# Second norm of an adaLN, attention and gated-MLP kernel: row groups 2 to 4 turned by VectorE block transposes and a trip through DRAM

## The chip, the cores and the metric

The kernel runs on one core of a Trainium2 chip. The metric is the device time of one execution in microseconds (us). The program is written by hand for five engines that each run their own queue in order: TensorE (PE: matmuls and transposes), VectorE (DVE), ScalarE (ACT), GpSimd (POOL) and SyncE (SP, which here issues nearly all DMA transfers). [...] PSUM is the memory that TensorE writes, SBUF the on-chip memory that all engines read, DRAM the memory outside.

## The reference, cut to what matters

Everything is fp32, with S = 2048 rows (tokens), D = 448 columns, 16 heads of 28, and FH = 896 hidden columns per half.

```python
mod = silu(c) @ w_mod                  # six parts of 448: sa, ca, ga, sb, cb, gb
h = layernorm(x) * (1 + ca) + sa       # first norm
x = x + ga * mha(h)                    # scores over all 2048 rows, softmax, wo
h = layernorm(x) * (1 + cb) + sb       # second norm
z = gelu(h @ w_in)                     # 2048 x 1792
z1, z2 = z[:, :896], layernorm(z[:, 896:])
g = w_sp @ z2 + b_sp[:, None]          # mixes the 2048 rows
x = x + gb * ((z1 * g) @ w_out)
```

## The kernel before, in words

An fp32 matmul is done as products of two fp32r parts: each operand is split into hi (a rounded copy, by ScalarE's `Copy`) and lo (the difference, by `sub`, L150). With D = 448, `h` transposed has 448 partitions' worth of rows in chunks of 128: chunks 0 to 2 have hi in slots 0 to 2 and lo in slots 3 to 5; the last 64 columns have hi in the lower and lo in the upper half of slot 6. For that, the last 64 columns are produced twice, in both halves of the partitions. A product over these slots is 11 matmuls, `STEPS`; its last two, `STEPS_Z = [(6, 6), (6, 7)]`, read slot 6.

The rows are handled as 16 tiles of 128 and 4 groups of 512 (`g`), four tiles each. The kernel goes through these stages: the first norm and the QKV products; attention; the output product wo; the second norm; z1 (the first half of h @ w_in, stored to DRAM); z2; the mix by w_sp; the gate and w_out (the y stage, where `x2_load`, L1508, fetches x back for the last addition).

The change lies between wo and z1. In this stretch there is no planner: the order of each engine's queue is the order in which the code calls the helpers, under a manual schedule.

- `x_load(g)` (L1037) loads a group of x, one DMA; the host lays out the inputs beforehand, so that partition p, tile t holds row g*512 + t*128 + p.
- `wo_tile(t)` is `wo_mm` (L830, 11 matmuls into PSUM) and `wo_add` (L1045, VectorE adds the product to x; L1046 stores the tile to `x2_scr`). For tiles 0 to 7 the two `STEPS_Z` matmuls and the add come later than the rest, in two loops.
- `h2_stats(g)` (L1054, L1058, L169, L170) takes mean and variance on VectorE and 1/sqrt(variance) on GpSimd.
- `h2_norm(g)` (L1066) normalises on VectorE, 448 columns and once more the last 64.
- `h2_group(g)` calls `ln_transpose`: 16 transposes on TensorE (L179, 4 chunks of 4 tiles), then for each chunk on ScalarE the scale and shift (L186, into `hfull`) and the hi copy (L193), and on VectorE the lo part (L150). The chunks are taken in the order 0, 2, 1, 3. `after(c)` is called behind each chunk.
- `z1_unit(g, f)` is 11 matmuls (L1158) into one PSUM bank, a gelu on ScalarE (L1162, which reads PSUM and writes one of four `z1t` slots), and a store (L1163). There are 28 units, four groups of seven; the units of group g read `h2T[g]`.
- `win_load` (L1074) and `win_prep` load and split w_in's second half for z2. `wout_load` (L1188), `wout_part` (L1192, L1194, L150) and `wout_store` (L1200) scale w_out by gb, split it and store it; for w_out chunk i they stand behind z1 units 10 + 2i, 11 + 2i and 12 + 2i.

The order is: statistics of groups 0 and 1, norm of group 0, tiles 8 to 11, norm of group 1, tile 12, transposes of group 0 (with tile 13 inside), tile 14, transposes of group 1 (with tile 15 and the statistics of group 2), norm of group 2, statistics of group 3, and the z1 units; group 2 is transposed behind unit 4, and group 3 behind unit 9.

## Time and profile before

| quantity | value |
|---|---|
| time of the kernel, median of 3 runs | 1376.16 us (1376.03 to 1377.29) |
| the profiled execution | 1376.63 us |
| its span in the profile | 1374.8 us |
| TensorE busy | 1368.6 us of the span |
| VectorE, ScalarE, GpSimd busy | 1112.7, 801.8, 359.6 us |
| moved by DMA | 254.32 MB, 185 GB/s on average |

The profile is of one execution. The span runs from its first to its last instruction, and the execution's own time is 1.8 us longer. Times within the trace are counted from the start of the span. A row that names an instruction has the line of the code, the engine, the operation, the tile written and the tiles read, and a count; "busy, mean ns" is the total time in us and the mean time of one, and what follows the second bar is the idle time of the engine ahead of these instructions with what ended it. In the chain of work and the timeline a row begins with the start and the duration in us. A row of a DMA queue has packets, MB, and the time they took as a share of all 16 DMA engines. PEclk is the clock granted to TensorE, in tenths, where 9 means 90% or more.

### The profile page before, as it was taken

What the parts mean: (1) busy time and instruction counts of PE and PEld (TensorE: products, weight loads), DVE (VectorE), ACT (ScalarE), POOL (GpSimd) and SP (SyncE); (2) the same over time, 40 slices, a digit from 0 to 9 for tenths busy, and PEclk for the clock granted to TensorE, in tenths of its full rate; (3) what the DMA queues carried; (4) which work ended last, traced back from release to release, by engine and by line L of the source; (5) the groups of instructions that cost most, each with busy time, mean ns of one, the idle gap of its engine ahead of it and who ended that gap; (6) DMA issues with size and microseconds to landing.
All of it is one profiled execution on the core that took longest, in us unless ns stands there. A gap on an engine that the chain in (4) does not pass through costs nothing.

```text
span 1374.8 us, 20854 instructions
## 1 busy us (share of the span) xinstructions
PE 1368.6 (100%) x7098; PEld 974.7 (71%) x7098; DVE 1112.7 (81%) x1771; ACT 801.8 (58%) x1471; POOL 359.6 (26%) x367
## 2 busy tenths in 40 slices
PE   9999999999999999999999999999999999999998
PEld 8888665556555655565556554888898888888898
DVE  7898899999999999999999981773367777999752
ACT  6623676767676767676767679364324544555420
POOL 2134335244535264745650012200011000000000
PEclk9999999999999999999999999999999999999999
DMA  8464756777677667776773110535604765788552
GB/s 289 137 175 176 233 158 214 201 221 229 210 218 209 209 203 237 234 224 214 231 221 103 32 44 23 177 139 179 225 20 142 233 203 184 249 283 267 180 183 90
DMA packets 137079, 254.32 MB, mean 185 GB/s; under 512 B 21832, under 2 KB 37322, under 8 KB 134426
## 3 DMA queue, kind: packets, MB, share of 16 engines
q1 hardware_dynamic: 134254, 248.79, 58.0%
q10 hardware_dynamic: 2718, 4.19, 0.8%
q8 instruction: 56, 0.92, 0.3%
q14 instruction: 51, 0.42, 0.1%
HBM read 174.53 MB, written 73.59 MB: 180 GB/s over the span
## 4 chain that ended last, share of the span: by engine, by line
PE 95%; DVE 2%; issue 2%; DMA 1%; POOL 0%; ACTq 0%; ACT 0%; DVEq 0%; POOLq 0%; SPq 0%
PE st_ps L743 18%; PE mt L711 17%; PE o_ps L758 16%; PE z_ps L1384 5%; PE acc L1453 5%; PE acc L1451 5%; PE acc L1452 5%; PE pq L406 5%; PE z_ps L1158 5%; PE pv L388 2%; PE y_ps L1518 2%; PE y_ps L1520 2%; PE y_ps L1519 2%; PE acc L1461 1%; PE acc L1459 1%
## 5 line engine op out<-in xcount | busy, mean ns | idle before, releaser
L716 DVE TENSOR_REDUCE pm<-mt 128x1 f32<-128x512 f32 x1024 | 627.4, 678 | 7.8 <-PE mt L711 7.8
L747 ACT ACTIVATE P<-st_ps 128x512 f32<-128x512 f32 x1024 | 512.6, 644 | 203.4 <-PE st_ps L743 200.9
L743 PE MATMUL st_ps<-qst,kst 128*128 128x512 f32 x1024 | 409.6, 410 | 0.0
L711 PE MATMUL mt<-kst,qst 128*128 128x512 f32 x1024 | 401.6, 392 | 0.0
L743 PEld LDWEIGHTS st_ps<-qst,kst 128*128 128x128 f32 x1024 | 191.2, 188 | 138.9 <-DVE pm L716 65.1
L758 PE MATMUL o_ps<-P,V 128*32 128x512 f32 x2048 | 240.0, 597 | 0.0
L711 PEld LDWEIGHTS mt<-kst,qst 128*128 128x128 f32 x1024 | 192.5, 188 | 34.7 <-ACT P L747 0.8
L868 POOL TENSOR_TENSOR ws_raw<-ws_raw 128x512 f32<-128x512 f32 x112 | 143.3, 1287 | 145.6 <-DMA ws_raw<-in_w_spT_dram 87.7
L1368 ACT ACTIVATE heapB<-raw_sp 128x512 fp32r<-128x512 f32 x156 | 96.9, 630 | 97.5 <-PE acc L1453 65.8
L758 PEld LDWEIGHTS o_ps<-P,V 128*32 128x32 f32 x2048 | 59.4, 109 | 126.8 <-issue 86.0
L1451 PE MATMUL acc<-heapB,heapA 128*128 128x512 f32 x312 | 121.4, 389 | 0.0
L1453 PE MATMUL acc<-heapB,heapA 128*128 128x512 f32 x312 | 121.4, 389 | 0.0
L764 DVE TENSOR_TENSOR osb<-osb,o_ps 128x512 f32<-128x512 f32 x82 | 56.4, 688 | 64.7 <-PE o_ps L758 63.3
L150 DVE TENSOR_TENSOR heapB<-raw_sp,heapB 128x512 fp32r<-128x512 f32 x112 | 74.5, 686 | 28.2 <-ACT heapB L1368 28.1
L1452 PE MATMUL acc<-heapB,heapA 128*128 128x512 f32 x222 | 86.5, 389 | 0.0
L1453 PEld LDWEIGHTS acc<-heapB,heapA 128*128 128x128 f32 x312 | 58.6, 188 | 12.2
L1451 PEld LDWEIGHTS acc<-heapB,heapA 128*128 128x128 f32 x312 | 58.6, 188 | 12.0
L406 PE MATMUL pq<-heapD,heapD 128*128 128x512 f32 x196 | 61.8, 390 | 0.0
L150 POOL TENSOR_TENSOR ws_raw<-ws_raw 128x512 fp32r<-128x512 f32 x44 | 56.7, 1288 | 3.5
L784 POOL TENSOR_TENSOR osb<-osb,rb 128x512 f32<-128x512 f32 x15 | 19.3, 1287 | 112.9 <-DMA rb<-r_scr 77.5
L1452 PEld LDWEIGHTS acc<-heapB,heapA 128*128 128x128 f32 x222 | 41.7, 188 | 8.9 <-DVE heapB L150 0.3
L170 POOL TENSOR_TENSOR rsz<-rsz,mhalf 128x1 f32<-128x1 f32 x16 | 14.2, 890 | 118.1 <-DVE rsz L169 118.1
(218 smaller groups left out, 1669.8 us busy)
## 6 DMA issues: line engine op xcount, KB each, us to landing
ws_raw<-in_w_spT_dram SPq DMA_DIRECT2D x136, 256.0 KB
ws_scr<-ws_raw SPq DMA_DIRECT2D x112, 256.0 KB
ws_raw<-ws_scr SPq DMA_DIRECT2D x88, 256.0 KB
raw_sp<-ws_scr SPq DMA_DIRECT2D x88, 256.0 KB
raw_sp<-in_w_spT_dram SPq DMA_DIRECT2D x68, 256.0 KB
wl_scr<-ws_raw SPq DMA_DIRECT2D x44, 256.0 KB
kst<-qk_scr SPq DMA_DIRECT2D x45, 224.0 KB
qst<-qk_scr SPq DMA_DIRECT2D x45, 224.0 KB
```

Of the source, the lines that this page charges most:

```text
L150: eng.tensor_tensor(out=dst, in0=a, in1=hi.bitcast(F32), op=ALU.subtract)
L406: pe.matmul(pq, wqk[:, b, m * 128 : (m + 1) * 128], hT[g][:, a, :], start=j == 0, stop=j == NST - 1)
L711: pe.matmul(mt, qst[h % 3][:, t * 128 : (t + 1) * 128], kst[h % 3][:, kb * 512 : (kb + 1) * 512], start=True, stop=True)
L716: dve.tensor_reduce(out=pms[h][:, t, kb : kb + 1], in_=mt, axis=AX.X, op=ALU.max)
L743: pe.matmul(st, kst[h % 3][:, kt * 128 : (kt + 1) * 128], qst[h % 3][:, qb * 512 : (qb + 1) * 512], start=True, stop=True)
L747: act.activation(p, st, AF.Exp, scale=SCALE)
L758: pe.matmul(o[32 * qb : 32 * qb + 32, :], V[:, u % NT, h, :], ptiles.pop((u, qb)), start=u == a, stop=u == e - 1)
L868: pool.tensor_tensor(out=a, in0=a, in1=b, op=ALU.add if W_SUMS[v][2] > 0 else ALU.subtract)
L1368: act.activation(hi, raw[0], AF.Copy)
L1451: pe.matmul(o, zh[:, c], hi, start=p < 2 and kt == 0, stop=False, skip_group_check=p > 1)
L1452: pe.matmul(o, zh[:, c], lo, start=False, stop=False, skip_group_check=p > 1)
L1453: pe.matmul(o, zl[:, c], hi, start=False, stop=kt == 3, skip_group_check=p > 1)
```

## The change

Lines behind the edits move in the changed kernel: `sub` is L151, the transposes L180, `hfull` L187, the hi copy L194, `wo_mm` L831, `wo_add` L1046 and L1047, the statistics L1055 and L1059, a z1 unit L1199, L1203 and L1204, w_in's load L1110, `wout_load` L1226, `wout_part` L1230 and L1232, and `wout_store` L1238. In it:

- For groups 1 to 3 (the diff counts from 0) the host lays out x in another order of rows, `rows_of`: tile t, partition 32a + i holds row g*512 + a*128 + t*32 + i. Attention runs over the rows in this order. `x2_load` brings back the order of rows in the y stage, by reading four runs of 32 rows for each tile of these groups.
- These groups are not transposed on TensorE. `h2_norm` normalises four tiles of 448 columns, `h2_turn` transposes them on VectorE in blocks of 32 by 32 (L1086), `h2_put` writes them to a scratch array of 448 x 512 in DRAM (four DMAs, L1090, in rows of 512 bytes), `h2_load` reads them back transposed into the lo slots of `h2T[g]` (three DMAs of 128x512 at L1102, and the last 64 columns twice at L1104), and `h2_group` makes from there `hfull` (L1187), hi (L1188) and lo (L151).
- The table `H2_AT` places these steps behind z1 units, counted 7g + f. Group 1: its turn is ahead of tile 15 and its put behind the transposes of group 0; load behind unit 1, `h2_group` behind units 3, 4 and 5. Group 2: statistics behind unit 0, norm 1, turn 2, put 3, load 5, `h2_group` 8 to 11. Group 3: statistics 4, norm 5, turn 6, put 7, load 9, `h2_group` 13 to 16.
- Group 0 keeps TensorE's transposes. Its statistics and norm come ahead of the second part of tiles 4 to 7; the norm is done by ScalarE (with a bias `nb3`, one VectorE instruction more), and the second copy of the last 64 columns by GpSimd. Its transposes stand behind tile 11, with tiles 12 to 15 called behind the four chunks.

```diff
@@ -112,6 +112,7 @@
     x2_scr = scr.tile([S, D], F32, name="x2_scr")
     z1_scr = scr.tile([FH, S], F32, name="z1_scr")
     ws_scr = scr.tile([4 * len(W_SUMS), 128, 512], F32, name="ws_scr")
+    hs_scr = [scr.tile([D, 512], F32, name=f"hs_scr{i}") for i in range(1, NG)]
     wo2_scr = scr.tile([2, 7, 128, D], F32, name="wo2_scr")
     wl_scr = scr.tile([2 * len(W_SUMS), 128, 512], F32, name="wl_scr")
 
@@ -1060,12 +1061,47 @@
 
     def h2_norm(g):
         mv, rs, _ = mv3.pop(g)
+        if g == 0:
+            nb = t3.tile([128, 4], F32, name="nb3")
+            dve.scalar_tensor_tensor(out=nb, in0=mv[:, :, 0], scalar=-1.0, in1=rs, op0=ALU.mult, op1=ALU.mult)
         for tt in range(4):
             xt = x3[4 * g + tt]
-            for o, i in ((xt[:, D:], xt[:, 384:D]), (xt[:, :D], xt[:, :D])):
+            if g == 0:
+                act.activation(xt[:, :D], xt[:, :D], AF.Identity, scale=rs[:, tt : tt + 1], bias=nb[:, tt : tt + 1])
+                pool.tensor_copy(xt[:, D:], xt[:, 384:D])
+            else:
                 dve.tensor_scalar(
-                    out=o, in0=i, scalar1=mv[:, tt, 0:1], scalar2=rs[:, tt : tt + 1], op0=ALU.subtract, op1=ALU.mult
+                    out=xt[:, :D], in0=xt[:, :D], scalar1=mv[:, tt, 0:1], scalar2=rs[:, tt : tt + 1], op0=ALU.subtract, op1=ALU.mult
                 )
+
+    blocks = {}
+
+    def h2_turn(g):
+        if g == 1:
+            b = fh.tile([128, 4 * 896], F32, name="turn", tag="heapE")
+        else:
+            b = t3.tile([128, 4, 512], F32, name="turn", tag="x3", bufs=3).rearrange("p a b -> p (a b)")
+        blocks[g] = b[:, 0:1792].rearrange("p (b t i) -> p b t i", t=4, i=32)
+        for tt in range(4):
+            dve.transpose(blocks[g][:, :, tt, :], x3.pop(4 * g + tt)[:, :D])
+
+    def h2_put(g):
+        for a in range(4):
+            sp.dma_start(
+                hs_scr[g - 1].rearrange("(b j) n -> j b n", j=32)[:, :, a * 128 : (a + 1) * 128],
+                blocks[g][32 * a : 32 * a + 32].rearrange("p b t i -> p b (t i)"),
+            )
+
+    heaps = []
+
+    def h2_load(g):
+        if g >= 2:
+            heaps.append(fh.tile([128, 4 * 896], F32R, name="heap", tag=("heapE", "heapC")[g - 2]))
+            h2T.append(hview(heaps[-1], 0, 7, 512))
+        for c in (0, 2, 1):
+            sp.dma_start(h2T[g][:, 3 + c, :].bitcast(F32), hs_scr[g - 1][c * 128 : (c + 1) * 128, :])
+        for r in (0, 64):
+            sp.dma_start(h2T[g][r : r + 64, 6, :].bitcast(F32), hs_scr[g - 1][384:D, :])
 
     raw_in = {}
 
@@ -1129,26 +1165,31 @@
         wo_mm(t, STEPS_Z)
         wo_add(t)
     o_split(3, 2, dve)
+    o_split(3, 3, dve)
+    h2_stats(0)
+    h2_norm(0)
     for t in range(4, 8):
         wo_mm(t, STEPS_Z)
         wo_add(t)
-    o_split(3, 3, dve)
-    h2_stats(0)
-    h2_stats(1)
-    h2_norm(0)
     heapF = dpool.tile([128, 4 * 896], F32R, name="heapF", tag="heapF")
     w2 = Halves(4, hview(heapD[2], 0, 4, 896), hview(heapF, 0, 4, 896))
     stg.close()
     t3b = ph3.enter_context(tc.tile_pool(name="t3b", bufs=2))
 
-    heaps = []
-
-    def h2_group(g, after=None):
-        if g >= 2:
-            heaps.append(fh.tile([128, 4 * 896], F32R, name="heap", tag=("heapE", "heapC")[g - 2]))
-            h2T.append(hview(heaps[-1], 0, 7, 512))
-        xns = [x3.pop(4 * g + t) for t in range(4)]
-        ln_transpose(xns, t3b, h2T[g], cols["cb"], cols["sb"], (act,) * 4, (dve,) * 4, None, after)
+    def h2_first(after):
+        xns = [x3.pop(t) for t in range(4)]
+        ln_transpose(xns, t3b, h2T[0], cols["cb"], cols["sb"], (act,) * 4, (dve,) * 4, None, after)
+
+    def h2_group(g, cs):
+        for c in cs:
+            f, hi = t3b.tile([128, 512], F32, name="hfull"), h2T[g][:, c if c < 3 else 6, :]
+            src = h2T[g][:, 3 + c, :].bitcast(F32)
+            act.activation(f, src, AF.Identity, scale=cols["cb"][:, c : c + 1], bias=cols["sb"][:, c : c + 1])
+            act.activation(hi, f, AF.Copy)
+            if c < 3:
+                sub(dve, h2T[g][:, 3 + c, :], f, hi)
+            else:
+                sub(dve, hi[64:128], f[64:128], hi[64:128])
 
     zbuf = []
 
@@ -1164,20 +1205,17 @@
 
     for t in range(8, 12):
         wo_tile(t)
-    h2_norm(1)
-    wo_mm(12, STEPS)
-    wo_add(12)
-    h2_group(0, lambda c: wo_tile(13) if c == 2 else None)
-    wo_tile(14)
-
-    def last_tile(c):
-        if c == 2:
-            wo_tile(15)
-        h2_stats(2, ((0, 2, 1, 3).index(c),))
-
-    h2_group(1, last_tile)
-    h2_norm(2)
-    h2_stats(3)
+        h2_stats(1, (t - 8,))
+
+    def late_tile(c):
+        if c == 3:
+            h2_turn(1)
+        wo_tile({0: 12, 2: 13, 1: 14, 3: 15}[c])
+        if c == 0:
+            h2_norm(1)
+
+    h2_first(late_tile)
+    h2_put(1)
     win_load(0, t3)
     win_load(1, t3b)
     wo3 = ph3.enter_context(tc.tile_pool(name="wo3", bufs=2))
@@ -1199,17 +1237,24 @@
         for i, part in enumerate(wouts.pop(f)):
             sp.dma_start(wo2_scr[i, f], part.bitcast(F32))
 
+    H2_AT = {}
+    for g, at_g in (
+        (1, ((1, h2_load), (3, h2_group, (0, 2)), (4, h2_group, (1,)), (5, h2_group, (3,)))),
+        (2, ((0, h2_stats), (1, h2_norm), (2, h2_turn), (3, h2_put), (5, h2_load))),
...
+    ):
+        for n, fn, *a in at_g:
+            H2_AT.setdefault(n, []).append((fn, g, *a))
     for g in range(NG):
         for f in range(7):
             z1_unit(g, f)
             for fn, n in ((wout_load, 10), (wout_part, 11), (wout_store, 12)):
                 if 0 <= 7 * g + f - n < 14 and (7 * g + f - n) % 2 == 0:
                     fn((7 * g + f - n) // 2)
-            if g == 0 and f == 4:
-                h2_group(2)
-                h2_norm(3)
-            if g == 1 and f == 2:
-                h2_group(3)
+            for fn, *a in H2_AT.get(7 * g + f, ()):
+                fn(*a)
             if g == 1 and f in (3, 5):
                 win_prep(f // 4, dve)
                 win_load(2 + f // 4, (t3, t3b)[f // 4])
@@ -1505,7 +1550,11 @@
 
     def x2_load(t):
         x2t[t] = wp.tile([128, 512], F32, name="x2l", tag="raw_sp", bufs=RAWS)[:, :D]
-        sp.dma_start(x2t[t], x2_scr[t * 128 : (t + 1) * 128, :])
+        g, a = divmod(t, 4)
+        if g == 0:
+            sp.dma_start(x2t[t], x2_scr[t * 128 : (t + 1) * 128, :])
+        else:
+            sp.dma_start(x2t[t], x2_scr.rearrange("(g t a i) d -> g a t i d", g=4, t=4, a=4)[g, a])
 
     def y_part(t, end=False):
         ts, uT = slice(t % 4 * 128, t % 4 * 128 + 128), uTs[t // 4]
@@ -1599,8 +1648,13 @@
         a = wm[k * 128 : min(k * 128 + 128, 448), i]
         return (a if k < 3 else a.transpose(1, 0, 2)).reshape(-1)
 
+    def rows_of(x):
+        first = x[:512].reshape(1, 4, 128, 448).transpose(0, 2, 1, 3)
+        later = x[512:].reshape(3, 4, 4, 32, 448).transpose(0, 1, 3, 2, 4).reshape(3, 128, 4, 448)
+        return _np.concatenate([first, later])
+
     lay = {
-        "x": _np.asarray(inputs["A_x"])[0].reshape(4, 4, 128, 448).transpose(0, 2, 1, 3),
+        "x": rows_of(_np.asarray(inputs["A_x"])[0]),
         "wqkv": twice(inputs["A_wqkv"]),
         "wo": twice(inputs["A_wo"]),
         "w_in": twice(inputs["B_w_in"]),
```

On TensorE, at the passage from wo to z1, the kernel before has (wo_ps is a tile of the wo product, tp a transpose, z_ps a z1 unit; the x names are the groups' tiles):

```order
L179 MATMUL tp<-ident,x_10443 128x128 x16
L830 MATMUL wo_ps<-heapD_91,heapD_89 128x448 x4
L830 MATMUL wo_ps<-heapD_91,heapD_90 128x448 x2
L830 MATMUL wo_ps<-heapD_91,heapD_89 128x448 x2
L830 MATMUL wo_ps<-heapD_91,heapD_90 128x448 x3
L1158 MATMUL z_ps<-heapB,heapA 128x512 x55
L179 MATMUL tp<-ident,x_10476 128x128 x16
L1158 MATMUL z_ps<-heapB,heapA 128x512 x55
L179 MATMUL tp<-ident,xl_10431 128x128 x16
L1158 MATMUL z_ps<-heapB,heapA 128x512 x44
```

The changed kernel has, at the same place, the end of tile 15 and then only z1 matmuls:

```order
L831 MATMUL wo_ps<-heapD_94,heapD_92 128x448 x4
L831 MATMUL wo_ps<-heapD_94,heapD_93 128x448 x2
L831 MATMUL wo_ps<-heapD_94,heapD_92 128x448 x2
L831 MATMUL wo_ps<-heapD_94,heapD_93 128x448 x3
L1199 MATMUL z_ps<-heapB,heapA 128x512 x154
L1199 MATMUL z_ps<-heap,heapA 128x512 x154
L1429 MATMUL z_ps<-heapD_94,heapB 128x448 x3
```

The three sets of 16 transposes behind tile 13 are no longer there; group 0's set stands in front of tile 12 now.

On SyncE, from the last x2 store on, the kernel before has (x_scr holds x for the y stage, z_scr is z1, raw_in a part of w_in, raw_out one of w_out):

```order
L1046 DMA x_scr<-xl_10431 128x448 x4
L1074 DMA raw_in<-in_w_in_dram 128x896 x2
L1163 DMA z_scr<-z1t 128x512 x11
L1188 DMA raw_out<-in_w_out_dram 128x448
L1074 DMA raw_in<-in_w_in_dram 128x896
L1163 DMA z_scr<-z1t 128x512 x2
L1188 DMA raw_out<-in_w_out_dram 128x448
```

The changed kernel has (turn holds a group's transposed blocks, hs_scr the scratch arrays, heapB and heap the `h2T` of groups 1, 2 and 3):

```order
L1047 DMA x_scr<-xl_10434 128x448 x4
L1090 DMA hs_scr_72<-turn 32x14x128 x4
L1110 DMA raw_in<-in_w_in_dram 128x896 x2
L1204 DMA z_scr<-z1t 128x512 x2
L1102 DMA heapB<-hs_scr_72 128x512 x3
L1104 DMA heapB<-hs_scr_72 64x512 x2
L1204 DMA z_scr<-z1t 128x512 x2
...
L1090 DMA hs_scr_74<-turn 32x14x128 x4
L1204 DMA z_scr<-z1t 128x512 x2
L1102 DMA heap<-hs_scr_74 128x512 x3
L1104 DMA heap<-hs_scr_74 64x512 x2
L1204 DMA z_scr<-z1t 128x512
L1226 DMA raw_out<-in_w_out_dram 128x448
```

The puts stand ahead of the w_in loads, the loads of a group between z1 stores, and the first w_out load stands behind the load of group 3.

On VectorE, from tile 15's x on, the changed kernel has (st is a tile's statistics, mv mean and variance, rs the factor; heapB is `h2T` of groups 0 and 1):

```order
L1046 TENSOR_TENSOR xl_10434<-xl_10434,wo_ps 128x448
L151 TENSOR_TENSOR heapB<-hfull,heapB 64x512
L1086 STREAM_TRANSPOSE turn<-x_10446 128x14x32 x4
L1046 TENSOR_TENSOR xl_10434<-xl_10434,wo_ps 128x448
...
L151 TENSOR_TENSOR heapB<-hfull,heapB 128x512 x3
L1055 BN_STATS st_10920<-xl_10434 128x6
...
L1059 BN_AGGR mv_10918<-st_10926 128x2
L170 TENSOR_SCALAR rs_10919<-mv_10918 128x4
L151 TENSOR_TENSOR heapB<-hfull,heapB 64x512
L1073 TENSOR_SCALAR xl_10434<-xl_10434,mv_10918,rs_10919 128x448 x4
L1086 STREAM_TRANSPOSE turn<-xl_10434 128x14x32 x4
```

The four transposes of group 1 stand between the last `sub` of group 0 and tile 15's add; the statistics of group 3 stand between the third and the last `sub` of group 1. Before, the order in the place of the first was:

```order
L1045 TENSOR_TENSOR xl_10431<-xl_10431,wo_ps 128x448
L150 TENSOR_TENSOR heapB<-hfull,heapB 128x512
L150 TENSOR_TENSOR heapB<-hfull,heapB 64x512
L1045 TENSOR_TENSOR xl_10431<-xl_10431,wo_ps 128x448
L150 TENSOR_TENSOR heapB<-hfull,heapB 128x512
L1054 BN_STATS st_10796<-x_10476 128x6
L150 TENSOR_TENSOR heapB<-hfull,heapB 128x512
L1045 TENSOR_TENSOR xl_10431<-xl_10431,wo_ps 128x448
L1054 BN_STATS st_10816<-x_10476 128x6
L150 TENSOR_TENSOR heapB<-hfull,heapB 128x512
```

There tile 15's add stood among the subs of group 1, and the statistics of group 2 behind it one tile at a time.

3 lines of the change are left out of this document (added).

## The prediction

> **What bounds the kernel now.** I began with the profile page, to see which engine carries the end.
>
> ```profile
> span 1374.8 us, 20854 instructions
> PE 1368.6 (100%) x7098; PEld 974.7 (71%) x7098; DVE 1112.7 (81%) x1771; ACT 801.8 (58%) x1471; POOL 359.6 (26%) x367
> PEclk9999999999999999999999999999999999999999
> PE 95%; DVE 2%; issue 2%; DMA 1%; POOL 0%; ACTq 0%; ACT 0%; DVEq 0%; POOLq 0%; SPq 0%
> ```
>
> TensorE is busy throughout at full clock and holds 95% of the chain that ended last. Work taken off TensorE is therefore gained, and any wait put into its queue is lost, one for one. Next I read the chain where the change acts:
>
> ```profile
> 898.35 1.93 PE tp L179 x16
> 900.28 2.24 PE wo_ps L830 x11
> 902.52 12.49 PE z_ps L1158 x55
> 915.01 1.75 PE tp L179 x16
> 929.25 1.75 PE tp L179 x16
> 931.00 44.90 PE z_ps L1158 x198
> ```
>
> The z1 stage is matmul without a gap: 55 matmuls in 12.49 us are five units of 2.50 us. Three sets of transposes (tp L179, 1.93, 1.75, 1.75) stand between them; group 0's stands ahead. Then the waits of TensorE in the stretch:
>
> ```profile
> PEld tp L179 <- DVE x L1066: 0.5, 1, 0.5
> PE tp L179 <- DVE x L1066: 0.3, 1, 0.3
> ```
>
> Apart from 0.5 and 0.3 us for group 0's norm, nothing holds TensorE here. So the whole price of the change lies in whether the new path for groups 1 to 3 delivers in time.
>
> **What comes off TensorE.** The 48 transposes of groups 1 to 3 go: 1.93 + 1.75 + 1.75 = 5.43 us. Group 0's norm now runs four tiles earlier, on ScalarE and GpSimd, beside the matmuls of tiles 4 to 11, so I take its 0.5 + 0.3 off too. Gain: 6.2 us (5.43 to 6.2). The first z1 unit starts at 902.52 less 1.93 less 0.8, about 899.75; unit n starts 2.50 us times n later, if nothing waits. Unit 7 is the first that reads group 1, unit 14 the first that reads group 2.
>
> **The new path, stage by stage.** The durations:
>
> ```profile
> L1054 DVE BATCH_NORM_STATS2 st<-x 128x6 f32<-128x448 f32 x12 | 6.9, 616 | 0.1
> L1066 DVE TENSOR_SCALAR x<-x,mv,rs 128x448 f32<-128x448 f32 x12 | 6.2, 513 | 0.4
> L1192 DVE TENSOR_TENSOR raw_out<-raw_out,bc_gb 128x448 f32<-128x448 f32 x7 | 4.4, 626 | 21.6 <-DMA raw_out<-in_w_out_dram 21.6
> L150 DVE TENSOR_TENSOR heap<-hfull,heap 128x512 fp32r<-128x512 f32 x6 | 4.2, 693 | 10.9 <-ACT heap L193 10.9
> L150 DVE TENSOR_TENSOR heapF<-raw_in,heapD 128x896 fp32r<-128x896 f32 x2 | 2.2, 1092 | 0.9 <-ACT heapD L157 0.9
> L1162 ACT ACTIVATE z1t<-z_ps 128x512 f32<-128x512 f32 x28 | 15.6, 590 | 11.1 <-PE z_ps L1158 11.1
> L186 ACT ACTIVATE hfull<-tp,col_sb,col_cb 128x512 f32<-128x512 f32 x16 | 12.2, 765 | 15.6 <-PE tp L179 12.4 <-DVE heapB L150 3.2
> L193 ACT ACTIVATE heap<-hfull 128x512 fp32r<-128x512 f32 x8 | 5.1, 632 | 0.7 <-ACT hfull L186 0.5
> L1194 ACT ACTIVATE wout<-raw_out 128x448 fp32r<-128x448 f32 x7 | 4.1, 579 | 27.1 <-issue 19.3 <-DVE raw_out L1192 7.8
> 914.97 0.36 DVE L1058 BATCH_NORM_AGGREGATE mv<-st 128x2 f32<-128x6 f32 x4
> 915.37 0.17 DVE L169 TENSOR_SCALAR rs<-mv 128x4 f32<-128x4 f32 x1
> ```
>
> Block transpose (L1086): not in the trace. Ends: 0.51 us, as the norm over the same 448 elements, and 1.09 us, as 896 elements (each element counted twice). I take 0.62, the statistics over 448 elements, the nearer kind of pass. A set of four is 2.5 us (2.0 to 4.4).
> [...]
>
> The stores and loads (L1090, L1102, L1104) pass through one queue:
>
> ```profile
> 836.57 0.33 SPq L775 DMA_DIRECT2D r_scr<-rt  x1
> 838.89 0.59 SPq L781 DMA_DIRECT2D rb<-r_scr  x1
> 876.48 0.64 SPq L1037 DMA_DIRECT2D xl<-in_x_dram  x1
> 905.44 0.92 SPq L1074 DMA_DIRECT2D raw_in<-in_w_in_dram  x2
> 936.98 0.33 SPq L1188 DMA_DIRECT2D raw_out<-in_w_out_dram  x1
> 939.60 0.63 DVE L1192 TENSOR_TENSOR raw_out<-raw_out,bc_gb 128x448 f32<-128x448 f32 x1 [1.44 <-DMA raw_out<-in_w_out_dram]
> 941.73 0.42 SPq L1188 DMA_DIRECT2D raw_out<-in_w_out_dram  x1
> 947.09 0.62 DVE L1192 TENSOR_TENSOR raw_out<-raw_out,bc_gb 128x448 f32<-128x448 f32 x1 [3.79 <-DMA raw_out<-in_w_out_dram]
> q1 hardware_dynamic: 562, 1.26, 81.2%
> q1 hardware_dynamic: 336, 0.46, 25.1%
> q1 hardware_dynamic: 64, 0.02, 4.1%
> ```
>
> The last three are queue rows of windows 908 to 912 (full load), 845.4 to 853.4 (stores from 28 partitions) and 824 to 826 (512-byte rows). Full load: 0.812 x 16 engines x 4 us = 52 engine-us for 1.26 MB, 388 GB/s over 16. A group is 0.92 MB in 1,792 rows of 512 bytes. Ends for four stores: 2.4 us at full rate, and 7.8 us. The upper one stacks two penalties: 512-byte rows cost 0.041 x 32 = 1.31 engine-us for 32 rows, 41 ns each (4.6 us for a group), and the partition scatter, 32.1 engine-us for 0.46 MB, is 1.7 times the full-load cost, so 70 ns. I take 45 ns, 5.0 us, since the rows' own size is the nearest likeness. Issuing a store that has many runs costs 0.62 us (xl, 0.64). A dependent transfer follows its store 2.3 us after the issue (836.57 to 838.89), about 0.85 us beyond its data.
>
> **Group 1, step by step.** Tiles 12 to 15 stay at 2.24 us. The sub of group 0's last column stands behind tile 14's add in DVE's order: tile 14 ends at 899.75 - 2.24 = 897.5, add and sub end at 898.9. Four transposes: to 901.4. Only then tile 15's add, to 902.0; its x2 store is queued on SyncE ahead of the puts, which are therefore issued from 902.4 to 904.9. Data from 903.2 to 908.3, landed at 909.1, and the loads wait for that. Ahead of them in the rings lie two w_in loads (0.92 MB, 2.4 us) and two z1 stores (1.3 us), with some 0.5 us to start, so to 912.5; the first chunk lands at 914.1. ScalarE then does four pairs (0.63 + 0.63) with two gelus (0.59) between: to 920.3. DVE takes three subs, but ahead of the last stand group 3's statistics (2.2 + 0.36 + 0.17 = 2.7): they start behind the third sub at 919.2, the last sub ends at 922.6. Unit 7 starts at 917.25 and reads that column in its last two matmuls, at 919.2. First wait: 3.4 us.
>
> **Group 2.** Unit 14 then starts at 938.15 and needs its last column at 940.1. Its own data are early; what is queued ahead is late. Norm(3) starts at 922.6 and takes 4 x 0.51, the transposes end at 927.3, the stores run to 933.7, landed 934.6, load(3) issues to 936.9. Behind load(3) on SyncE stand a z1 store and the first w_out load (L1226), issued at 937.4. Such loads took 939.60 - 936.98 = 2.6 and 947.09 - 941.73 = 5.4 us before; I take 4.3, with load(3)'s 0.92 MB ahead. Landed 941.7, DVE mult 0.63, ScalarE w_out 0.58, group 2's last pair 1.26, sub 0.69: 944.9. Second wait: 4.8 us. With two waits behind it, group 3 has about 3 us to spare.
>
> **At nothing.** The norms of group 0 on ScalarE and the GpSimd copies lie beside tiles 4 to 11, the VectorE work removed there (12 copies of 64 columns) beside the same; if that cover failed, up to the 0.8 us above returns. z1 stores held behind load(1) and load(3) on SyncE cost nothing while ScalarE has a free z1t slot (four of them, 2.5 us each). The x2 loads in four runs keep their 1,792-byte rows and lead their adds:
>
> ```profile
> L1508 SPq DMA_DIRECT2D x2l<-x_scr x16: 319/320/446, 1289.1 to 1345.8; - x16
> L1523 DVE TENSOR_TENSOR x2l<-x2l,y_ps x17: 380/614/622, 1307.4 to 1371.5; 128x448 f32<-128x448 f32 x15, 128x224 f32<-128x224 f32 x2
> ```
>
> The first issue is 18 us ahead of the first add, the last 26; without that lead each of 12 loads could cost the 0.3 us by which 0.64 exceeds 0.32.
>
> **The sum.** -6.2 + 3.4 + 4.8 = +2.0 us. The profiled execution lasted 1376.63 us (span 1374.8 plus 1.8), 0.47 above the median of the runs, 1376.16. So the median becomes 1378.2. Varying one term at a time through the same steps: stores at 21 ns a row -3.5, at 70 ns +10; transposes at 0.51 us +1.3, at 1.09 us +4.9; ScalarE's f at 0.77 us (L186) +0.5 on each wait. All at their best: -6; the worst stores and transposes together: +12.
>
> **Rivals.** B, faster: the trip is in time for both groups. This needs the path 3.4 us shorter for group 1, as with stores at the full-load rate, or loads that are not served behind the w_in loads. Speaking for it: 388 GB/s over the neighbouring window; against: every small-row window is slower, and the w_out load that took 5.4 us stood behind other transfers. Time: -3.5 to -6.2, so 1370.0 to 1372.7.
> C: only the first wait is real, because the w_out load lands in 2.6 us or DVE gets its work from ScalarE in another overlap; -6.2 + 3.4 = -2.8, about 1373.4, up to 1374.5.
> D, slower: stores at 70 ns a row. It decides above about 50 ns, where each further 10 ns adds some 1.1 us to a group's stores and moves both waits; at 70 ns +10, so 1381 to 1388. The 28-partition scatter speaks for it, the 512-byte rows alone against. A second way to the same times is a clock that drops in the waits. The page shows PEclk 9 in every slice, but also no TensorE wait over 1.0 us here, so it cannot tell. [...]
>
> **How the numbers follow.** This kernel's runs cannot tell changes under 0.2% (2.75 us) from none, so 1373.4 and 1378.9 are the borders. A, both waits, 0.48, own range 1375.5 to 1382: 0.26 of it slower, 0.22 same. D 0.18, slower. C 0.12: 0.08 same, 0.04 faster. B 0.22: 0.20 faster, 0.02 same. Together faster 0.24, same 0.32, slower 0.44. For 8 in 10 the range reaches into B and D: 1370.8 to 1386.
>
> **What would show it.** In the profile after: tp L180 with 16 instructions in this stretch, not 64; z1 matmuls waiting for DVE's sub (L151) once near 919 (3 us) and once near 940 (5 us), never at unit 21; L1086 near 0.62 us; the put's data about 5 us; the first h2 load's ScalarE activation near 914; stats(3) between the last two subs of group 1. I am wrong if TensorE waits at neither place (B), if the second wait is missing (C), if L1086 is over 0.9 us or the stores pass 6 us (D), or if PEclk falls below 9 behind the waits.

## The result, and the profile after

The changed kernel takes 1383.53 us (median of 4 runs, 1383.31 to 1385.3) against 1376.72 us before (4 runs beside it). The ratio is 1.0051, with a 95% interval of 1.0034 to 1.0069: some 7 us slower, clear of the 0.2% below which the forecast took a change for none. The forecast was 1378.2 us, slower by 2. The range 1370.8 to 1386 holds the result, but the range of the case forecast, 1375.5 to 1382, does not: 1383.5 lies among the times given to rival D.

The profile after, from its page (first the span and the busy times, then the granted clock in 40 slices, then the chain's shares):

```profile
span 1381.6 us, 20787 instructions
PE 1368.9 (99%) x7050; PEld 973.5 (70%) x7050; DVE 1113.8 (81%) x1764; ACT 805.1 (58%) x1475; POOL 361.3 (26%) x371
PEclk9999999999999999999999999999999999999999
PE 94%; DMA 2%; DVE 1%; issue 1%; SPq 1%; ACT 0%; POOL 0%; ACTq 0%; DVEq 0%; POOLq 0%
```

There are 48 TensorE instructions fewer (7098 to 7050), as the diff says, and DMA now has 2% of the chain. That TensorE's busy time did not fall with them is the first hint: some of its instructions became slower. The page's 40 slices are 35 us wide and hide it.

TensorE's timeline shows where. First before, then after; each row has its start, its duration, the count, and in brackets the idle time ahead of it with what ended it:

```profile
866.13 0.94 PE L1114 MATMUL sums<-osum,spread 128*128 128x512 f32 x2
902.35 12.66 PE L1158 MATMUL z_ps<-heapB,heapA 128*128 128x512 f32 x55
975.73 0.77 PE L1384 MATMUL z_ps<-heapD,heapB 128*128 128x448 f32 x3
```

```profile
867.03 0.93 PE L1150 MATMUL sums<-osum,spread 128*128 128x512 f32 x2
889.89 1.91 PE L180 MATMUL tp<-ident,x 128*128 128x128 f32 x16
900.54 17.86 PE L1199 MATMUL z_ps<-heapB,heapA 128*128 128x512 f32 x78
919.00 1.42 PE L1199 MATMUL z_ps<-heapB,heapA 128*128 128x512 f32 x5 [0.60 <-ACT heapB L1188]
920.85 1.23 PE L1199 MATMUL z_ps<-heapB,heapA 128*128 128x512 f32 x3 [0.43 <-ACT heapB L1188]
924.89 18.46 PE L1199 MATMUL z_ps<-heapB,heapA 128*128 128x512 f32 x68 [2.82 <-DVE heapB L151]
943.19 2.20 PE L1199 MATMUL z_ps<-heap,heapA 128*128 128x512 f32 x9
948.21 34.59 PE L1199 MATMUL z_ps<-heap,heapA 128*128 128x512 f32 x145 [2.82 <-DVE heap L151]
982.64 0.77 PE L1429 MATMUL z_ps<-heapD,heapB 128*128 128x448 f32 x3
```

A matmul of z1 takes 0.227 us at full clock (12.49 us for 55 in the chain before). With that the rows can be read as an account of the 6.8 us between the spans:

| part | before | after | difference |
|---|---|---|---|
| start of the span to the `sums` matmul (end of attention) | 866.13 | 867.03 | +0.9 |
| `sums` to the first z1 matmul | 36.22 | 33.51 | -2.7 |
| first z1 matmul to the first z2 matmul | 73.38 | 82.10 | +8.7 |
| z2 to the end | 399.07 | 398.96 | -0.1 |

The z1 stage lost 3.5 us of transposes, so its 82.1 us are 12.2 above the 69.9 of its matmuls. Unit 7's last two matmuls (the head of the row at 924.89) would have started at 900.54 + 86 x 0.227 = 920.1: 4.8 us late, in three pieces of which the last is the sub of the last column. The last two of unit 14 would have started at 943.19 + 9 x 0.227 = 945.2 and started at 948.2: 3.0 us late. The rest is in the rows' lengths. 68 matmuls from 924.89 to 943.19 took 18.3 us and need 15.4; 145 from 948.21 to 982.64 took 34.4 and need 32.9. That is 2.9 and 1.5 us. The windows there show why; the columns are the busy time of each engine with its count, then the granted clock, the DMA share and GB/s:

```profile
920.00:925.00 5.00, 1.76 (x6) 0.59 (x4) 3.94 (x11) 3.07 (x6) 0.73 (x1) 0.89 0.81 235
925.00:930.00 5.00, 5.00 (x12) 3.93 (x13) 4.26 (x8) 0.60 (x1) 1.55 (x2) 0.50 0.78 257
930.00:935.00 5.00, 5.00 (x21) 4.05 (x21) 0.94 (x2) 3.48 (x6) 0.00 (x0) 0.92 0.66 155
945.00:950.00 5.00, 2.18 (x6) 1.49 (x5) 2.86 (x4) 3.72 (x6) 0.00 (x0) 0.78 0.42 138
950.00:955.00 5.00, 5.00 (x21) 4.01 (x20) 1.94 (x3) 3.09 (x5) 0.00 (x0) 0.88 0.86 264
```

Behind each wait the granted clock is down, to 0.50 from 925 to 930: TensorE is "busy" there, with 12 matmuls where 5 us hold 22.

What stands ahead of the waits is in the chain of the changed kernel (pieces of it, in order of time):

```profile
903.01 0.42 SPq L1090
909.44 6.57 DMA heapB<-hs_scr
916.10 0.83 ACT hfull L1187
920.83 0.69 DVE heapB L151
921.52 2.12 DVE st L1055 x4
...
924.27 1.45 POOL rs L171
925.74 2.38 DVE xl L1073 x4
...
928.60 1.66 DVE turn L1086 x3
930.28 0.32 SPq L1090
932.03 5.20 DMA hs_scr<-turn
937.32 0.32 SPq L1102
940.45 0.38 SPq L1226
940.92 4.99 DMA raw_in<-in_w_in_dram
945.98 0.81 ACT hfull L1187
948.21 34.59 PE z_ps L1199 x145
```

This is the path of the forecast: put, load behind the queue, ScalarE, then statistics ahead of the last sub; and for the second wait the norm, turn and put of group 3 (its norm behind a step on GpSimd, L171, that the forecast has not), its load, the first w_out load (L1226, issued at 940.45), and then group 2's last column. The piece at 940.92 bears the name of the w_in load that was issued right after it; VectorE's timeline names the w_out load itself:

```profile
944.83 0.62 DVE L1230 TENSOR_TENSOR raw_out<-raw_out,bc_gb 128x448 f32<-128x448 f32 x1 [5.00 <-DMA raw_out<-in_w_out_dram]
```

### The profile page after: what moved, and what is told of

Same layout as the page of the kernel before. It is cut to its first block, busy times and chain, and to the rows that moved or that the text cites. A ratio compares the mean times of both kernels' runs of the same rounds, so it can differ in the third digit from the quotient of the medians.

```text
span 1381.6 us, 20787 instructions
## 1 busy us (share of the span) xinstructions
PE 1368.9 (99%) x7050; PEld 973.5 (70%) x7050; DVE 1113.8 (81%) x1764; ACT 805.1 (58%) x1475; POOL 361.3 (26%) x371
## 4 chain that ended last, share of the span: by engine, by line
PE 94%; DMA 2%; DVE 1%; issue 1%; SPq 1%; ACT 0%; POOL 0%; ACTq 0%; DVEq 0%; POOLq 0%
PE st_ps L744 18%; PE mt L712 17%; PE o_ps L759 16%; PE z_ps L1429 5%; PE acc L1497 5%; PE acc L1496 5%; PE acc L1498 5%; PE pq L407 5%; PE z_ps L1199 3%; PE wo_ps L831 2%; PE pv L389 2%; PE y_ps L1568 2%; PE y_ps L1569 2%; PE y_ps L1567 2%; PE acc L1504 1%
## 5 line engine op out<-in xcount | busy, mean ns | idle before, releaser
L151 DVE TENSOR_TENSOR heapB<-raw_sp,heapB 128x512 fp32r<-128x512 f32 x112 | 74.6, 688 | 28.0 <-ACT heapB L1413 27.9
L1498 PEld LDWEIGHTS acc<-heapB,heapA 128*128 128x128 f32 x312 | 58.6, 188 | 12.2
L1496 PEld LDWEIGHTS acc<-heapB,heapA 128*128 128x128 f32 x312 | 58.6, 188 | 12.2
L151 POOL TENSOR_TENSOR ws_raw<-ws_raw 128x512 fp32r<-128x512 f32 x44 | 56.7, 1288 | 3.5
L171 POOL TENSOR_TENSOR rsz<-rsz,mhalf 128x1 f32<-128x1 f32 x16 | 14.2, 890 | 116.0 <-DVE rsz L170 116.0
```

Source lines behind the costliest of these rows:

```text
L151: eng.tensor_tensor(out=dst, in0=a, in1=hi.bitcast(F32), op=ALU.subtract)
L1496: pe.matmul(o, zh[:, c], hi, start=p < 2 and kt == 0, stop=False, skip_group_check=p > 1)
L1498: pe.matmul(o, zl[:, c], hi, start=False, stop=kt == 3, skip_group_check=p > 1)
```

## The experiments

In all of them the kernel before was run beside the changed one; its median was 1375.97 to 1376.23 us. Because attention's end moves from execution to execution (below), I compare single profiles by the time from `sums` to the end of the span (before 508.7 us, after 514.6) and from z1 to z2 (69.9 us where nothing waits and nothing but z1 runs).

**No dependency on the trip.** The z1 units of groups 1 to 3 read group 0's columns.

```diff
-            pe.matmul(ps_t, ..., h2T[g][:, a, :], ...)
+            pe.matmul(ps_t, ..., h2T[0][:, a, :], ...)
```

> The changed kernel, with the z1 units of groups 1 to 3 reading group 0's columns, so that no z1 unit waits for the trip through memory; all other work stays, and z1 is computed from the wrong rows. Theory (all of the loss is TensorE's two waits and the half clock behind them): z1 is gapless at 2.50 us a unit and the kernel takes 1376.7 - 6.2 = 1370.5 us (1369.5 to 1371.7). Rival (the added DMA traffic, ScalarE and GpSimd work, or attention in the other row order cost something by themselves): 1373 us or more.

Measured: 1380.78 us (1378.51 to 1382.42), ratio 1.0032 (1.0019 to 1.0045), 10 us above the theory. The number is the rival's, but its cause is another: the gain up to z1 is there (33.5 us from `sums`), and no unit waits for the trip, but TensorE waits all the same, and later (76.1 us from z1 to z2, and 403.8 to the end). Its waits in this kernel's stretch from 895 to 1010 (time in all, times, longest):

```profile
PE z_ps L1199 <- ACT z1t L1203: 4.8, 5, 1.5
PE z_ps L1429 <- ACT z1t L1203: 2.7, 2, 2.1
```

It waits for gelus, that is for free PSUM banks, and the waits of ScalarE and the issues on SyncE say what ScalarE was doing:

```profile
ACT wout L1232 <- DVE raw_out L1230: 23.0, 5, 12.7
```

```profile
939.77 0.38 SPq L1226 DMA_DIRECT2D raw_out<-in_w_out_dram  x1
948.45 0.42 SPq L1226 DMA_DIRECT2D raw_out<-in_w_out_dram  x1
...
972.93 0.42 SPq L1226 DMA_DIRECT2D raw_out<-in_w_out_dram  x1
```

From the second to the sixth (948.45 to 972.93, four steps) the w_out loads go out 6.1 us apart, while two z1 units, which belong to each of them, take 5.0. So I had missed a second bound: the w_out steps form a loop, in which a load stands on SyncE behind two z1 stores, the stores wait for gelus, and the gelus stand on ScalarE behind the w_out step before. If the first load is late (939.77), the seven steps end behind z1: here the last load goes out at 978.11, 2.9 us behind the first z2 matmul. In the kernel before the steps are as long (5.9 us), but the last load goes out at 972.72, 3.0 us ahead of z2, and nothing waits. The last two kernels below test this.

**Filling the waits.** Spare matmuls on group 0's data, ahead of the last two of units 7 and 14. First 11 at each place:

```diff
         for j, (a, b) in enumerate(STEPS):
+            if j == NST - 2 and 7 * g + f in (7, 14):
+                spare = bank("spare")
+                for _ in range(11):
+                    pe.matmul(spare, w1[:, 0, 0:128], h2T[0][:, 0, :], start=True, stop=True)
             pe.matmul(ps_t, ...)
```

> The changed kernel, with 11 matmuls into a spare PSUM bank (about 2.5 us, the result is not read) ahead of the last two matmuls of units 7 and 14, where the two waits of 2.8 us stand. Theory (the clock is halved because TensorE idles): the granted clock stays at or near 1.00 behind both places, the waits are no longer than before, and the time falls by 2.8 + 1.5 = 4.3 us to about 1379.2 (1378.3 to 1380.5). Rival (the matmuls behind the waits are slow for another reason, such as DMA traffic on the same memory): the units behind stay slow and the time stays at 1383.5, or rises by the matmuls' own time.

Measured: 1383.65 us (1382.32 to 1385.9), no gain, where the theory had 1379.2. But the timeline holds both halves of the answer:

```profile
920.54 2.68 PE L1202 MATMUL spare<-heapB,heapA 128*128 128x512 f32 x11
923.52 15.71 PE L1203 MATMUL z_ps<-heapB,heapA 128*128 128x512 f32 x68 [0.29 <-DVE heapB L151]
941.11 2.65 PE L1202 MATMUL spare<-heapB,heapA 128*128 128x512 f32 x11
947.73 35.78 PE L1203 MATMUL z_ps<-heap,heapA 128*128 128x512 f32 x145 [3.96 <-DVE heap L151]
```

At the first place the same 68 matmuls take 15.7 us in place of 18.5: the granted clock was 1.00 from 920 to 940. Unit 14 then comes 2.6 us earlier, counted from the first z1 matmul, but its column does not, so that the 11 spare matmuls leave 4.0 us idle, and the clock falls there, to 0.65 from 945 to 950 and 0.67 from 950 to 955. Then 11 and 28:

> The changed kernel with 11 spare matmuls ahead of unit 7's last two and 28 (6.4 us) ahead of unit 14's. In the run with 11 and 11 the 68 matmuls behind the first place took 15.7 us in place of 18.3, while the second wait had grown and left 4.0 us idle, with 145 matmuls in 35.8 us behind it where full clock needs 33.0. Theory (idle time of some 3 us is what lowers the clock): with the second place filled as well the granted clock stays near 1.00 throughout, the 145 matmuls take 33.0 us, and the time is 1383.65 - 2.8 = 1380.8 (1379.8 to 1382). Rival (the second slowdown comes from the DMA traffic there): 1383.6 as before.

Measured: 1381.74 us (1380.74 to 1383.29). The 145 matmuls:

```profile
947.65 33.16 PE L1203 MATMUL z_ps<-heap,heapA 128*128 128x512 f32 x145
```

33.2 us in place of 35.8 and, in the changed kernel, 34.6, with like DMA traffic (from 950 to 955, 263 GB/s against 258 and 264) and a granted clock of 1.00 there against 0.67 and 0.88. So the slow matmuls are the idle time's doing, and not the transfers'. The waits remain, since spare work is no work: z1 to z2 is 81.1 us. That is only 1.0 us below the changed kernel's 82.1, though the account above put 2.9 + 1.5 us down to the slow clock: unit 14 comes earlier, its column does not, and the time saved ahead of it is spent in front of it.

**The first wait alone.** Three edits: the w_in loads behind units 2 and 3, put(1) ahead of tile 15's store, and the statistics of group 3 behind group 1's last sub.

```diff
-    win_load(0, t3)
-    win_load(1, t3b)
...
+            if g == 0 and f in (2, 3):
+                win_load(f - 2, (t3, t3b)[f - 2])
...
             h2_turn(1)
+            h2_put(1)
...
-        (3, ((4, h2_stats), (5, h2_norm), ...
+        (3, ((5, h2_stats), (5, h2_norm), ...
```

> The changed kernel, with only the path of group 1 shortened: the two w_in loads issued behind z1 units 2 and 3 and so behind load(1), put(1) issued ahead of tile 15's x2 store, and the statistics of group 3 behind group 1's last sub. Theory (the first wait is the put, the queue behind the w_in loads, and the statistics): no wait at unit 7, which needs its last column at 920.1 and gets it at about 919.5. The second wait does not depend on the first and its data come at about 944.5 while unit 14 now asks at 937.6, so it grows from 3.0 to about 6.9 us: 1383.5 - 4.8 - 2.8 + 3.9 + about 0.7 for a longer time at half clock = 1380.5 (1379 to 1382). Rival (the second wait moves with the first, since the chain behind it starts at the first): it stays at 3.0 us, 1375.9.

Measured: 1380.53 us (1380.32 to 1381.81). The theory's 1380.5 is met to a tenth, in part by luck: z1 to z2 is 80.7 us, only 1.4 below the changed kernel's, and the other 1.5 of the 3.0 us come from attention, which ended 1.5 us earlier in this profile (865.5 against 867.0). The wait at unit 7 is gone, and the second has grown:

```profile
899.06 35.08 PE L1199 MATMUL z_ps<-heapB,heapA 128*128 128x512 f32 x154
944.88 35.04 PE L1199 MATMUL z_ps<-heap,heapA 128*128 128x512 f32 x145 [8.70 <-DVE heap L151]
```

14 units without a gap, and then 8.7 us idle and 2 us of slow clock (0.50 granted from 940 to 945, 0.61 from 945 to 950). Removing one wait let the other grow, to more than the 6.9 I had worked out: counted from the first z1 matmul, group 2's last column came 1.9 us earlier than in the changed kernel, and not the 3.7 of the forecast. Put(3) and the first w_out load behind it were issued 2.7 us earlier, but that load took 5.2 us from its issue to VectorE in place of 4.4; why was not tested.

**The second wait alone.** The w_out loads one unit earlier, so that the first stands ahead of load(3).

```diff
-            for fn, n in ((wout_load, 10), ...
+            for fn, n in ((wout_load, 9), ...
```

> The changed kernel, with the w_out loads issued behind z1 units 9, 11, ... in place of 10, 12, ..., so that the first one stands ahead of load(3) on SyncE, and nothing else moved. Theory (the second wait is the first w_out load held behind put(3) and load(3)): the wait at unit 14 and the low clock behind it go, 1383.5 - 3.0 - 1.5 = 1379.0 (1378.3 to 1380). Rival (group 2's own data are late): no change, 1383.5.

Measured: 1376.6 us (1375.2 to 1380.38), ratio 1.0003 (0.9994 to 1.0013), below the theory's range. There is no wait left at unit 14 (154 matmuls in 35.07 us from 944.72), only the first with its slow clock (0.55 granted from 925 to 930). From `sums` to the end it is 509.8 us, 4.8 below the changed kernel, as expected (4.5). The median fell by 6.9 against the changed kernel's. This path does not explain the 2 us more. The profiled execution, at 1380.38, was the slowest: it reached `sums` 1.8 us later than the changed kernel's, and the start of an execution moves by such amounts (last section). Its mean granted clock was 0.995, that of the other nine 0.997 to 0.999, and that of the changed kernel's four 0.994 or 0.995. So the others kept more of the clock, at the start or behind the first wait; which, no trace shows.

**Which of the three edits shortens the first wait.** Both kernels have the w_out loads one unit earlier; one moves only the statistics, the other only the w_in loads.

> The w_out loads one unit earlier, and the statistics of group 3 behind group 1's last sub; the w_in loads stay ahead of load(1). Theory: the last sub follows its hi copy at once, which takes about 1.5 us off the first wait of 4.8; 1376.6 - 1.5 = 1375.1, or 1372.3 if the shorter wait also spares the clock. Rival (the queue behind the w_in loads is all that counts): 1376.6, no change.

Measured: 1378.71 us (1376.28 to 1380.72), no gain but 2 us more than the kernel with the w_out loads alone, as neither the theory nor the rival had it. The first wait did shrink, its last piece from 2.82 to 1.34 us, and the clock behind it was 1.00 (from 920 to 940); but then unit 14 came earlier, and group 3's statistics later, so that the second wait is back, with 3.6 us and a low clock (0.83 from 940 to 950).

> The w_out loads one unit earlier, and the two w_in loads issued behind units 2 and 3, so behind load(1); the statistics of group 3 stay ahead of the last sub. Theory (transfers are served in the order of issue, so 0.92 MB ahead cost 2.4 us): the first chunk of group 1 comes some 2.5 to 3 us earlier, near 913 on the clock of the changed kernel's trace, and the first wait falls to about 2 us: 1376.6 - 2.7 = 1373.9, or 1371 if the clock holds. Rival (the loads are not served behind the w_in loads): chunk at the same time, 1376.6.

Measured: 1373.84 us (1372.68 to 1374.84), ratio 0.9981 (0.9972 to 0.999), as expected. Here are the two waits that remain:

```profile
920.30 15.72 PE L1199 MATMUL z_ps<-heapB,heapA 128*128 128x512 f32 x68 [1.65 <-DVE heapB L151]
939.28 33.16 PE L1199 MATMUL z_ps<-heap,heapA 128*128 128x512 f32 x145 [1.22 <-DVE heap L151]
```

So load(1) had waited for the w_in loads issued ahead of it: the first chunk of group 1 reached ScalarE 2.8 us behind the first issue of load(1) (908.72 to 911.51), and 6.7 us in the changed kernel (909.44 to 916.10). The 0.92 MB of w_in ahead of load(1) were the main part of the first wait (unit 7's last two matmuls are 1.8 us late now, 4.5 in the kernel with the w_out loads alone). And around 1.65 and 1.22 us of idle time the granted clock stayed at 1.00 (from 900 to 950): 15.7 us for 68, 33.2 for 145.

**Both paths mended.** The edits of the first-wait and of the second-wait kernel together.

> The edits of the first-wait and the second-wait run together: w_in loads behind load(1), put(1) ahead of tile 15's x2 store, statistics of group 3 behind group 1's last sub, and the w_out loads one unit earlier. Theory (the two waits and the low clock behind them are the whole loss, and the run without a dependency lost its gain to the w_out loads held behind load(3)): no wait in z1, full clock, 1376.0 - 6.2 = 1369.8 us (1368.8 to 1371.3). Rival (with the waits gone the next queue becomes late: the w_out loads or group 3's data): a wait of 1 to 4 us between units 10 and 24, 1371 to 1376.

Measured: 1375.05 us (1374.16 to 1376.56), ratio 0.9991 (0.9982 to 1.0): the rival came true. A wait of 2.9 us stands at unit 14. The chain leads through the first w_out load: issued at 931.79, behind put(3) and two z1 stores, 3.9 us to landing.

```profile
931.79 3.88 DMA raw_out<-in_w_out_dram
...
936.84 0.81 ACT hfull L1187
938.33 0.70 DVE heap L151
939.07 34.54 PE z_ps L1199 x145
```

One unit earlier is not enough, since put(3) waits on SyncE for its transposes. So the first two w_out loads go behind units 6 and 7, ahead of put(3); with all the other edits, and with the w_in move alone:

```diff
+                if fn is wout_load and 7 * g + f in (6, 7):
+                    fn(7 * g + f - 6)
...
+                    if fn is not wout_load or 7 * g + f >= 14:
```

> The run with both paths mended kept a wait of 2.9 us at unit 14: the first w_out load was issued at 931.7, still behind put(3), and landed at 935.7. Here the first two w_out loads are issued behind units 6 and 7, ahead of put(3); the other edits stay (w_in loads behind load(1), put(1) ahead of tile 15's x2 store, statistics of group 3 behind group 1's last sub). Theory (what is left is put(3) ahead of the w_out load): no wait in z1, full clock, 1376.2 - 6.2 = 1370.0 us (1369 to 1371.5). Rival (a wait of about 3 us comes back at unit 14 from load(2) or at unit 21 from group 3's data): 1372 to 1375.

> Only the order on SyncE is changed against the changed kernel: the w_in loads behind load(1), the first two w_out loads ahead of put(3). The statistics of group 3 stay ahead of group 1's last sub, put(1) behind tile 15's x2 store. Theory: the first wait is 1.7 us as in the run with the w_in loads moved, the second is none, and no wait is long enough for the clock: 1376.2 - 6.2 + 1.9 = 1371.9 us (1370.8 to 1373). Rival (the second wait there was put(3)'s own lateness): 1.2 us more, 1373.1 or above, no gain over 1373.8.

Measured: 1370.61 us (1369.64 to 1371.26), ratio 0.9955 (0.9942 to 0.9967), and 1372.0 us (1371.73 to 1374.98), ratio 0.997 (0.9959 to 0.9982). Both as the theory had them. The first has one wait of 0.59 us in z1, 70.7 us from z1 to z2, and is faster than both kernels, 5.5 us below the kernel before: most of the 6.2 us that the forecast took off TensorE was real. The second kernel differs from the changed one in the order on SyncE alone, and from `sums` to the end it takes 504.8 us in place of 514.6: that order had cost more than the whole gain.

**Group 1 back on TensorE.** Groups 0 and 1 by transposes (16 of them behind unit 2), 2 and 3 by the trip, the first two w_out loads early.

```diff
-        (1, ((1, h2_load), (3, h2_group, (0, 2)), (4, h2_group, (1,)), (5, h2_group, (3,)))),
+        (1, ((2, h2_second),)),
...
-        if c == 3:
-            h2_turn(1)
...
-        first = x[:512].reshape(1, 4, 128, 448).transpose(0, 2, 1, 3)
+        first = x[:1024].reshape(2, 4, 128, 448).transpose(0, 2, 1, 3)
```

> Group 1 goes back to TensorE's transposes (behind unit 2, ahead of its use at unit 7) and to rows in plain order; groups 2 and 3 keep the trip through memory, and the first two w_out loads are issued ahead of put(3). Theory: the first wait is gone with its cause, TensorE pays 1.75 us for 16 transposes: 1376.2 - 6.2 + 1.75 = 1371.8 us (1370.8 to 1373). Rival (groups 2 and 3 alone still make TensorE wait, at units 14 or 21): 1374 or more.

Measured: 1376.29 us (1373.39 to 1378.35), a miss of 4.5 us, and by neither wait that I had named. z1 ran without one. The loss is in z2: 404.1 us from z2 to the end in place of 399.0, where TensorE first waits 2.1 us for a gelu (and the clock falls to 0.89 from 975 to 990). From the third on, the w_out loads of this kernel went out at 944.2, 953.9, 959.9, 965.7 and 971.0: the loop seen in the first run. The steps are as long in the kernel with all the edits (943.0 to 969.4), whose last load goes out 1.1 us ahead of the first z2 matmul, and it lost nothing; here it is 0.2 us. The last kernel opens the loop, with three buffers and the third to the seventh load four units earlier than in this one, behind units 10 to 18 in place of 14 to 22 (the expectation says two units for every load; the edit moves these five by four, and the first two stay):

```diff
+                    elif 7 * g + f in (10, 12, 14, 16, 18):
+                        fn((7 * g + f - 6) // 2)
...
-        wouts[f] = [wo3.tile([128, D], F32, name="raw_out")]
+        wouts[f] = [wo3.tile([128, D], F32, name="raw_out", bufs=3)]
```

> The run with group 1 on TensorE, and every w_out load two z1 units further ahead of its use, with three buffers in place of two. In that run TensorE waited nowhere in z1, but the w_out steps came every 6 us while two z1 units take 5.0: each load stood on SyncE behind two z1 stores, which wait for gelus, which stand on ScalarE behind the w_out step before; the last ended after z1 and held up z2. Theory (this loop costs the 4.5 us by which the run missed): with the loads ahead the steps keep up with the units, z2 starts without a wait, and the time is 1371.8 us (1370.8 to 1373). Rival (the loss in z2 has another cause, such as the w_out stores or the clock alone): 1375 or more.

Measured: 1372.43 us (1371.32 to 1374.2), ratio 0.997 (0.9958 to 0.9981). The last load goes out at 956.9, z1 to z2 takes 71.6 us, the 1.75 of the transposes included, and z2 to the end is 399.0 again. So the late w_out steps were the cause of the miss; the earlier loads and the third buffer were not tried apart. That they were also the cause of the loss in the first run rests on that run's waits and issues; this edit was not tried there.

## Why the prediction was right or wrong

**Right, with its sizes.** What comes off TensorE: -2.7 us up to z1 (forecast 1.93 + 0.8) and 3.5 in z1. The block transpose:

```profile
L1086 DVE STREAM_TRANSPOSE turn<-x 128x448 f32<-128x448 f32 x8 | 4.4, 614 | 0.0
```

0.61 us against 0.62 taken. The stores: from the first issue of put(3), 930.28, to the issue that waits for its landing, 937.32, are 7.0 us (forecast 927.3 to 934.6, 7.3), and 512-byte rows moved at some 177 GB/s, 46 ns a row and engine (45 taken):

```profile
GB/s 35 12 0 0 29 187 170 178 176 184 178 167 176 178 178 167 190 158 135 132 275 295 263 249 225 222 258 167 158 208 217 184 184 164 211 199 345 416 351 386
```

(The rate from 930.3 to 937.3 in 40 slices; the sixth to the 17th are the put alone, and z1 stores are issued from then on.) Both waits are at the two units forecast, unit 21 has none, and the x2 loads in four runs cost nothing (z2 to the end is unchanged to 0.1 us), nor do the norms of group 0 (the stretch up to z1 is shorter by the whole 2.7 us).

**Right in mechanism, off in size.** The first wait is 4.8 us and not 3.4. The first chunk reached ScalarE 15.6 us behind the first z1 matmul, not 14.4, and ScalarE's scale and shift from SBUF took 0.80 us and not 0.63: I had taken the copy's row where the nearer one was the same instruction reading PSUM, 0.77. The second wait is 3.0 and not 4.8, though its column came 2.5 us later than forecast (47.7 us behind the first z1 matmul, not 45.2); unit 14 came later still, since the first wait had grown and the slow clock had put 2.9 us on top. A wait is the difference of two times, and both moved.

**The step that failed** is the sum: "-6.2 + 3.4 + 4.8 = +2.0 us". Its two waits make 8.2 us, while z1 took 12.2 us more than its matmuls need: waits of 4.8 and 3.0, and 2.9 and 1.5 us of slow clock behind them. With -6.2 that makes +6.0, and with 0.9 us from the start of the execution the profile's 6.8 is accounted for to 0.1. The forecast had the clock only as the second way of rival D, with no run to give it a size, because no wait of TensorE before was longer than 1.0 us.

But not all of the 4.4 us of slow clock is a loss. Unit 14's last two matmuls start when group 2's last column is there, whatever TensorE did before, and with the clock kept up in both places z1 to z2 still took 81.1 us. The first wait and the slow clock behind it were hidden by the second wait. So what the sum lacked in z1 is 4.0 us of two kinds: 1.5 of slow clock behind the last wait, and the 2.5 by which the column was late. That lateness builds up along the path: 1.2 us at the first chunk of group 1 on ScalarE, 1.5 at the statistics of group 3, and 2.3 at the norm of group 3, which the forecast started right behind the last sub, though it waits for GpSimd's 1/sqrt (L171, 1.45 us). That step was left out of the forecast without a reason.

The clock itself was halved behind the first wait (0.50 granted from 925 to 930) and came back as TensorE worked on (0.92 from 930 to 935, then 1.00). Idle pieces of 2.8 us were enough, twice in the changed kernel and once (2.9, with 0.93 granted from 930 to 940 and 0.90 from 940 to 950) in the kernel with both paths mended, and 1.65 us was not (1.00). The work behind the two waits took 2.9 and 1.5 us more.

**Missed altogether:** the loop of the w_out loads, at 6 us a step against 5.0 us of TensorE. It can be read in the trace of the kernel before, where the loads go out 5.9 us apart from 949 to 973. I priced the first of them, and not their period. In the changed kernel it costs nothing, since its waits put z2 off (last load at 978.6, z2 at 982.6).

**Rivals.** B's case (the trip in time for both groups) was made by hand, by four edits, and gave its time, 1370.6 against "1370.0 to 1372.7". C, in which the second wait is hidden, is the kernel with the early w_out load, 1376.6 rather than 1373.4, since the first wait was short by 1.4 us and the clock was not in the sum. D's first way, stores at 70 ns a row, is refuted by the 46 ns; its second way, the clock, is there, and together with the late column and the slow start of the execution it carries the time out of A's range, though A's two waits came where they were forecast. That the whole range holds the result is owed to its reach into D.

## What to carry to other kernels

When work leaves the engine that bounds a kernel for a longer path on other engines, price the last place where the bound engine may wait not only by the wait, but also by the slower clock behind it (here 1.5 us behind a wait of 3.0; the 2.9 us behind the earlier wait cost nothing, since the later wait hid them), and ask of every transfer on the new path which queue it joins, what is ahead of it, and who stands behind it. The two waits in a row hid each other here: removing the first, which was 7.7 us with its slow clock, made z1 only 1.4 us shorter, because the second grew by 5.8 and the slow clock behind it by 0.5; so mend them together, and check periodic chains (here a w_out step every 6 us) against the new, faster pace. Moving two pairs of loads on SyncE made a change that lost 7 us one that gained 4; two more edits made it gain 5.5.

## What the runs showed of the hardware

- Idle pieces of 2.8 us and longer on TensorE lowered the granted clock, to between 0.50 and 0.93 over the windows of 5 or 10 us around them, and the work behind took 1.5 to 2.9 us more; pieces of 1.2 to 1.7 us did not (1.00). In the run with no dependency and in that with group 1 on TensorE a wait of 2.1 us went with a clock of 0.89 over the 15 us around it. Filling the idle time with spare matmuls kept the clock at 1.00 (11 and 28 of them, from 915 to 960).
- Attention, which the change reaches only by the order of rows, ended at 866.1 us of the span in the profile of the kernel before, at 867.0 in the changed kernel's, and at 868.9 in that of the kernel with the w_out loads one unit earlier. The clock granted over the first 20 us was 1.00, 0.91 and 0.83, in this order. The first and the last row (the clock is the third column from the end):

```profile
0.00:20.00 20.00, 18.54 (x108) 16.29 (x109) 14.57 (x47) 10.24 (x21) 4.57 (x11) 1.00 0.89 337
```

```profile
0.00:20.00 20.00, 17.46 (x98) 16.10 (x98) 12.13 (x40) 8.99 (x19) 3.74 (x10) 0.83 0.90 337
```

Other profiles of kernels in the same order of rows reached this point at 865.5 to 866.6 (the one above 866 with a clock of 0.91, the others with 1.00), so the order is not the cause. Why the clock differs at the start was not tested. For single profiles it is safer to compare stages than spans.
